# Pairs of steps on TensorE in batches 1 to 3, with batch 0 in float32r throughout

## The chip, the cores and the metric

The kernel runs on one core of one Trainium2 chip. The metric is the time of one execution in device microseconds, measured several times on the chip, with the median taken. A profiled execution is one more execution, whose instructions were recorded; its own time lies among those of the others.

## The reference

`x` has 4 batches of 12416 rows of 128; `inducing` has 32 rows of 128. Each batch goes through two attentions and then through a gated feed-forward part:

```
h   = softmax(inducing @ x.T / sqrt(128)) @ x          # 32 x 128
a   = softmax(x @ h.T / sqrt(128))                     # 12416 x 32
y   = a @ h                                            # 12416 x 128
out = (silu(y @ w_gate) * (y @ w_val)) @ w_out         # w_gate, w_val 128 x 1536, w_out 1536 x 128
```

All data is float32.

## The kernel before

**Tiling.** The 12416 rows of a batch are cut into 25 columns (`COLS`, line 43). Column 0 and the columns of the first three groups have 512 rows, 13 columns in all; the other 12 have 480. The 1536 hidden units are 12 tiles of 128. One **slot** is one tile `t` of one column `c`, so a batch has 300 slots and the kernel 1200. The weights of gate and value are multiplied by `h` beforehand (`proj_round`), so a slot's operand is the softmax itself, laid out as a stack of four 32-row groups (`stack`, 128 x 512).

**A slot.** `front` (line 774) issues two float32r matmuls on TensorE (PE), the gate `g` (line 787) and the value `v` (line 788), each into a PSUM bank of its own from the pool `ps_gv`, which has 6. `gate` (793) makes the silu of `g` on ScalarE (ACT). `value` (801) multiplies it with `v` on VectorE (DVE). The product `h` goes to SBUF (pool `hp`, 3 buffers), except for the tiles in `DVE_TILES` = {1, 5, 9} (in the last batch `LAST_DVE` = {1, 7}), where it overwrites `v` in PSUM. `split` (803) cuts `h` into a rounded high part (a cast, line 814, on ACT, or on DVE for tile 11; in the last batch for tiles 5 and 11) and the rest (a subtraction, line 816, on GpSimd (POOL), or on DVE for the tiles whose `h` lies in PSUM). `back` (820) issues three matmuls `o` into an accumulator from `ps_o` (2 banks): low weights by high part (831), high weights by high part (832), high weights by low part (833). After tile 11 `evac` (837) copies the accumulator on DVE (line 841 or 843) and stores it.

**Types.** From column `CSW` = 13 of batch 0 on (`u.half`, line 778) the two parts and the output weights are float16; before it they are float32r. Float16 needs scales. `peak_of`, `peak_a` to `peak_d` find bounds of the weights, `half_a` to `half_c` make the float16 output weights, `size_a` to `size_d` find each batch's scale, and `rise` (line 474) multiplies batch 0's value weights by the scale, since they were made without it. All this runs as extra steps in slots of batch 0, from the constants in line 63: `WPK` = 104 (bounds), `WSZ` = 128 (scale), `WOH` + 10 = 144 (float16 weights), and slot 146 on for `rise`.

**Order of the work.** The program is unrolled and the order written is the order on each engine. The main loop (lines 881 to 906) does, for each slot: `front`, `gate`, `value` of this tile, then `split` of the tile before it (kept in `wait`), then the extra steps that are due, then `back` of the oldest tiles until no more than `ahead` tiles lie between `front` and `back`. `ahead` is `SKEW` = 5 and rises to `HI` = 10 while the next batch's attention is in the making; at a slot in `bursts`, where ACT computes a long exponential, the tile is split at once and `ahead` falls back, so that PE has a stock of `o` matmuls to work on. The attention of batch b+1 is spread as steps over the slots of batch b (`plan`, line 653). A step whose accumulator comes from `ps_o` has `acc` and waits until the running accumulator isn't about to change (line 899).

Of the kernel before, what the change touches and what calls it, by code (L numbers as in the profile page):

```python
# [9 lines left out]
F32 = mybir.dt.float32  # L10
# [3 lines left out]
ALU = mybir.AluOpType  # L14
AX = mybir.AxisListType
# [27 lines left out]
COLS = [(0, 0)] + [(q, j) for q in range(1, NF) for j in range(NG)]  # L43
SLOTS = len(COLS) * NT
NXT = 4
HI = 10
RAMP = 6
BF = (2, 3, 11, 10)
SKEW = 5
# [10 lines left out]
E0 = 36  # L60
TINY = 2.0 ** -50
LAST_DVE, LAST_CAST = {1, 7}, {5, 11}
WPK, WSZ, WOH, CSW = 104, 128, 134, 13

# [43 lines left out]
def induced_set_attention_then_swiglu(ctx: ExitStack, tc: tile.TileContext, xt, xn, ind, wgv, wo, out):  # L110
# [63 lines left out]
    nc.gpsimd.memset(wide, 2.0 ** 127)  # L174
    peak = const.tile([P, 12], F32, name="peak")
    top = const.tile([P, 36], F32, name="top")
    peaks = const.tile([P, P], F32, name="peaks")

    def floor2(out, in_):

        nc.vector.tensor_scalar(out=out.bitcast(U32), in0=in_.bitcast(U32), scalar1=0x7F800000, scalar2=None, op0=ALU.bitwise_and)
# [7 lines left out]
        at = 6 * k + i  # L189
        nc.vector.tensor_reduce(out=peak[:, at:at + 1], in_=w[:, WP * i:WP * i + WP], op=ALU.max, axis=AX.X, apply_absolute_value=True)  # L190

    def peak_a(k):
        nc.vector.tensor_reduce(out=peak[:, 10 + k:11 + k], in_=peak[:, (0, 6)[k]:(6, 9)[k]], op=ALU.max, axis=AX.X)
        nc.vector.tensor_scalar(out=peaks, in0=ones, scalar1=peak[:, 10 + k:11 + k], scalar2=None, op0=ALU.mult)

    def peak_b(k):
        ps = ps_gv.tile([P, 512], F32, name="gv")
        nc.tensor.matmul(out=ps[:, 0:P], lhsT=peaks, rhs=ident, start=True, stop=True)
        nc.vector.tensor_scalar(out=peaks, in0=ps[:, 0:P], scalar1=TINY, scalar2=None, op0=ALU.max, op1=ALU.max, accum_out=top[:, k:k + 1])

    def peak_c():
        floor2(top[:, 1:2], top[:, 1:2])
        inverse2(top[:, 2:3], top[:, 1:2])

# [5 lines left out]

    def half_a(i):
        cs = slice(WP * i, WP * i + WP)
        joint[i] = sgl.tile([P, WP], F32, name="joint%d" % i)
        nc.gpsimd.tensor_add(out=joint[i], in0=wo_hi[:, cs].bitcast(F32), in1=wo_lo[:, cs].bitcast(F32))

    def half_b(i):
# [53 lines left out]
    def attention(b, one, xn0=None, xt0=None):  # L270
# [180 lines left out]
            nc.vector.tensor_scalar(out=st.hV.bitcast(U32), in0=st.hT[:, 0:M].bitcast(U32), scalar1=0x7FFFFFFF, scalar2=None, op0=ALU.bitwise_and)  # L451

        def size_b():
            ps = ps_gv.tile([P, 512], F32, name="gv")
            nc.tensor.matmul(out=ps[:, 0:M], lhsT=ones, rhs=st.hV, start=True, stop=True)  # L455
            st.sc = att.tile([P, 8], F32, name="sc")
            c = lambda i: st.sc[:, i:i + 1]
            st.up, st.down = c(0), c(1)
            nc.vector.tensor_reduce(out=c(2), in_=ps[:, 0:M], op=ALU.max, axis=AX.X)
            nc.vector.tensor_scalar(out=c(3), in0=c(2), scalar1=top[:, 0:1], scalar2=TINY, op0=ALU.mult, op1=ALU.max)  # L460
            floor2(c(4), c(3))
            inverse2(c(5), c(4))
# [7 lines left out]

        def size_d():
            nc.vector.tensor_scalar(out=st.hV, in0=st.hT[:, 0:M], scalar1=st.up, scalar2=None, op0=ALU.mult)

        def rise(i):

            v = st.w[:, WP * i + 2 * P:WP * i + 4 * P]
            nc.gpsimd.tensor_mul(out=v, in0=v.bitcast(F32), in1=st.up.broadcast_to([P, 2 * P]))

        def weights():
            if not hasattr(st, "w"):  # L480
# [172 lines left out]
    def plan(st, p):  # L653

        f, s = st.f, []

        def add(slot, step, *args):
            def go():
                f[step](*args)


            go.acc = (NT - 1, 0, 1) + (2,) * (step == "hacc") if step in ("s1", "max_b", "hacc", "h_c", "s2") else ()
            s.append((slot, go))

        def blocks(q):
            return CH0[q], CH0[q] + CH[q]

        last = p["S1"][0] + p["S1"][1] * (NCH - 1)
        v1 = last - 3 * p["S1"][1]
        for q in range(NCH):  # L670
            add(p["LX"][0] + p["LX"][1] * q if q < NXT else v1 + 1 + 3 * (q - NXT), "load_xt", q)

            add(v1 if q < NXT else last, "s1", q, q not in (0, NXT))
        mb = last + p["MX"]
        add(last + 2, "max_a"), add(mb, "max_b")
        e1 = mb + p["E1"]
        for q in range(NXN):
            add(e1 - p["LN"][0] + p["LN"][1] * q, "load_xn", q)
            add(e1, "exp1_part", q)
            add(e1, "eT", q)  # L680
            add(e1 + p["HA"][q], "hacc", q, (0, NXN - 1))
        add(e1, "exp1_part", NXN, NCH - 1)
        for q in range(NXN, NCH):
            k = NXN + (q - NXN | 1)
            at = e1 + p["HB"][0] + p["HB"][1] * (k - NXN)
            add(max(at - p["HC"][0] - k + q, e1 + 1 + (p["HB"][0] + p["HB"][1] if q == NCH - 1 else p["HA"][0])), "load_xn", q)
            add(at - p["HC"][1] + 1 - k + q, "eT", q)
            add(at, "hacc", q, (k - 1, k))
        add(at, "h_a")
        add(at + 2, "h_b")  # L690
        hn = at + p["HD"]
        add(hn, "h_c")
        for i, step in enumerate(("size_a", "size_b", "size_c", "size_d")):
            add(hn + 3 * i + 2, step)
        for i, q in enumerate(S2O):
            k = i % NXT
            at = hn + 4 + p["H2"] * (NXT - 1) if i < NXT else hn + p["H2"] * (NCH - 1)
            add(at, "s2", *blocks(q), i not in (0, NXT))
            if i + NXT < NCH:
                add(at + 1, "load_xt", S2O[i + NXT])  # L700
            d = 2 if i < NXT else 1
            add(at + 1 + d * k, "s2_max", *blocks(q))
            add(at + 3 + (d + 1) * k, "s2_sub", *blocks(q))
        e2 = at + 4 + p["E2"]
        add(e2, "exp2")
        st.e1, st.bursts = e1, {e1, e2}
        for i in range(2):
            add(e2 + p["PR"][0], "proj_round", i)
            for k in range(NG * NG):
                add(e2 + p["PR"][i] + 3 + k * p["PQ"], "proj_spread", i, k // NG, k % NG)  # L710
        for q in range(NF):
            first = [u for u, (p, j) in enumerate(COLS) if p == q][0]
            s += post(st, q, nc.gpsimd, SLOTS + NT * (first - NST) + 2, SLOTS)
        return sorted(s, key=lambda x: x[0])
# [146 lines left out]
    for b in range(B):  # L861
        nxt = attention(b + 1, (one, oneb)[(b + 1) % 2]) if b + 1 < B else None
        if nxt is not None:
            nxt.steps = plan(nxt, PA if b == 0 else PB)
            if b == 0:
                cur.steps.append((nxt.e1, lambda: run(f"e2:52:{NTB}")))
                for q in range(2, NF):
                    base = NT * (1 + NG * (q - 1) - NST) + 2
                    base = max(base, E0 + 4) if q < 4 else max(base, nxt.e1 + 1)
                    cur.steps += post(cur, q, nc.gpsimd, base)  # L870
                once = [lambda x=(k, i): peak_of(*x) for k in range(2) for i in range((6, 3)[k])]
                once += [lambda: cur.f["size_a"](), lambda: peak_a(0)]
                cur.steps += [(WPK + 2 * i, f) for i, f in enumerate(once)]
                once = [lambda: peak_b(0), lambda: peak_a(1), lambda: cur.f["size_b"](), lambda: peak_b(1), peak_c, peak_d, cur.f["size_c"]]
                cur.steps += [(WSZ + 2 * i, f) for i, f in enumerate(once)]
                cur.steps += [(WOH + 10 + 2 * i, lambda i=i: (half_a, half_b, half_c)[i // 3](i % 3)) for i in range(9)]
                cur.steps += [(NT * (CSW - 1) + 2 * i + 2, lambda i=i: cur.f["rise"](i)) for i in range(6)]
                cur.steps.sort(key=lambda x: x[0])
        bursts = (nxt.bursts if nxt is not None else set()) | ({E0} if b == 0 else set())
        last_burst = max(bursts, default=0)  # L880
        for slot in range(NT if b == 0 else 0, SLOTS):
            c, t = slot // NT, slot % NT
            u = front(cur, b, c, t)
            gate(u)
            value(u)
            u.cast_dve = t in (LAST_CAST if b == B - 1 else CAST)
            u.last = b == B - 1 and slot == SLOTS - 1
            if wait:
                split(wait[0])
                pend.append(wait.pop(0))  # L890
            wait.append(u)
            if slot in bursts:
                u.cast_dve = True
                split(u)
                pend.append(wait.pop(0))
            for a in (cur, nxt):
                while a is not None and a.steps and a.steps[0][0] <= slot:

                    if pend and pend[0].t in getattr(a.steps[0][1], "acc", ()):
                        break  # L900
                    a.steps.pop(0)[1]()
            ahead = min(ahead + 1 / RAMP, HI) if nxt is not None and slot < last_burst else max(ahead - 1 / RAMP, SKEW)
            if slot in bursts:
                ahead = SKEW - (b == 0)
            while len(pend) + len(wait) > ahead:
                back(pend.pop(0))
        if nxt is not None:
            nxt.steps = [(at - SLOTS, f) for at, f in nxt.steps]
        cur = nxt
# [41 lines left out]
```

## Time and profile before

| | |
|---|---|
| median of 3 runs | 1452.67 us (1452.27 to 1453.83) |
| the profiled execution | 1453.71 us, of which the span from first to last instruction is 1451.9 us |
| mean granted TensorE clock | 0.995 |
| first matmul of batch 0, 1, 2, 3 on line 787 | 38.8, 417.8, 767.2, 1116.5 us from the start of the span |

An instruction's row gives its engine, its line in the kernel, what it writes and reads by tile names, its shapes, how many there were, their busy time and the mean of one in ns, and the idle time just before them with what ended it. Matmuls overlap: the spacing of their starts, not their length, is what one costs in a stream. On ACT and DVE too, the next instruction's start may lie up to 0.1 us before the recorded end of the one before.

### The profile page before, as it was taken

The page shows a single profiled execution, that of the slowest core. Times are in us where ns is not written, and L with a number is a line of the kernel's source. Part 1 is how long each engine was busy: PE and PEld are TensorE (multiplying, and loading weights), DVE is VectorE, ACT ScalarE, POOL GpSimd, SP SyncE. Part 2 cuts the span into 40 slices and gives each one's busy share as a digit, 9 for nine tenths or more (in the row PEclk, how much of TensorE's full clock was granted, in tenths as well). Part 3 has the DMA queues.
Part 4 walks back from the last instruction along what each step waited for, and adds up shares of the span by engine and source line. Part 5 has one row for each costly group of instructions (what it writes and reads, how often), then busy time and mean ns, then how long its engine had stood idle before and what let it go on. Part 6 is the DMA issues. An engine that isn't in the chain of part 4 may idle for free.

```text
span 1451.9 us, 25130 instructions
## 1 busy us (share of the span) xinstructions
PE 1434.0 (99%) x7512; PEld 825.1 (57%) x7512; DVE 1208.2 (83%) x2138; ACT 1266.5 (87%) x2366; POOL 1139.7 (78%) x1036
## 2 busy tenths in 40 slices
PE   9999998999999999999999999999999999999999
PEld 6577776555555555555555455455555555555554
DVE  6888878988888879888888878978888878888887
ACT  4889787789998788899999888799999898889897
POOL 1689768778788667787888767778878889889887
PEclk9999999999999999999999999999999999999999
DMA  9233522212132532121114324221111111111110
GB/s 373 63 98 119 180 87 85 96 52 76 32 111 76 185 129 106 52 70 41 42 36 144 129 88 137 106 74 49 39 42 43 32 42 45 31 44 39 41 42 21
DMA packets 50824, 119.82 MB, mean 83 GB/s; under 512 B 11392, under 2 KB 28288, under 8 KB 50688
## 3 DMA queue, kind: packets, MB, share of 16 engines
q1 hardware_dynamic: 50688, 118.22, 25.0%
q8 instruction: 59, 0.97, 0.3%
q14 instruction: 77, 0.63, 0.1%
HBM read 62.87 MB, written 25.43 MB: 61 GB/s over the span
## 4 chain that ended last, share of the span: by engine, by line
PE 81%; ACT 0%; DVE 0%; issue 0%; DVEq 0%
PE o L831 16%; PE gv L788 16%; PE gv L787 16%; PE o L833 15%; PE o L832 15%; PE gv L329 1%; PE o L377 1%; PE o L329 1%; PE gv L511 0%; ACT silu L793 0%; ACT h_hi L814 0%; DVE ob L841 0%; PE gv L390 0%; PE o L443 0%; PE gv L455 0%
## 5 line engine op out<-in xcount | busy, mean ns | idle before, releaser
L816 POOL TENSOR_TENSOR h_lo<-h,h_hi 128x480 f16<-128x480 f32 (+2 forms) x915 | 1035.4, 1153 | 262.8 <-ACT h_hi L814 185.3
L793 ACT ACTIVATE silu<-gv 128x512 f32<-128x512 f32 (+1 forms) x1200 | 702.8, 587 | 96.4 <-PE gv L787 73.5
L801 DVE TENSOR_TENSOR h<-gv,silu 128x512 f32<-128x512 f32 (+1 forms) x916 | 610.5, 668 | 185.0 <-ACT silu L793 126.3
L787 PE MATMUL gv<-stack,tw 128*128 128x512 f32 (+1 forms) x1200 | 654.1, 545 | 2.2 <-DVE h L801 1.0
L814 ACT CAST h_hi<-h 128x480 f16<-128x480 f32 (+2 forms) x788 | 475.2, 603 | 52.0 <-DVE h L801 45.8
L788 PE MATMUL gv<-stack,tw 128*128 128x512 f32 (+1 forms) x1200 | 466.6, 389 | 3.2 <-DVE h L801 2.3
L831 PE MATMUL o<-h_hi,wo_l 128*128 128x480 f16 (+1 forms) x1044 | 399.0, 382 | 0.0
L832 PE MATMUL o<-h_hi,wo_h 128*128 128x480 f16 (+1 forms) x1044 | 388.2, 372 | 0.0
L833 PE MATMUL o<-h_lo,wo_h 128*128 128x480 f16 (+1 forms) x1044 | 388.2, 372 | 0.0
L787 PEld LDWEIGHTS gv<-stack,tw 128*128 128x128 f32 x1200 | 227.7, 190 | 129.1 <-ACT tw L501 2.7
L831 PEld LDWEIGHTS <-wo_l 128*128 128x128 f16 x1044 | 100.3, 96 | 266.1 <-issue 260.9
L788 PEld LDWEIGHTS gv<-stack,tw 128*128 128x128 f32 x1200 | 227.7, 190 | 39.2 <-ACT silu L793 7.5
L801 DVE TENSOR_TENSOR gv<-gv,silu 128x512 f32<-128x512 f32 (+1 forms) x272 | 184.5, 678 | 30.7 <-ACT silu L793 28.8
L816 DVE TENSOR_TENSOR h_lo<-gv,h_hi 128x480 f16<-128x480 f32 (+2 forms) x272 | 181.0, 665 | 1.4
L833 PEld LDWEIGHTS <-wo_h 128*128 128x128 f16 x1044 | 102.2, 98 | 114.3
L814 ACT CAST h_hi<-gv 128x480 f16<-128x480 f32 (+2 forms) x269 | 153.0, 569 | 10.2 <-DVE gv L801 8.5
L832 PEld LDWEIGHTS <-wo_h 128*128 128x128 f16 x1044 | 104.8, 100 | 3.5
L841 DVE TENSOR_SCALAR ob<-o,sc 128x480 f32<-128x480 f32 (+1 forms) x87 | 62.9, 723 | 0.5 <-PE o L833 0.5
L814 DVE CAST h_hi<-h 128x480 f16<-128x480 f32 (+2 forms) x128 | 61.6, 482 | 0.0
L831 PE MATMUL o<-h_hi,wo_lo 128*128 128x512 f32 x144 | 57.8, 402 | 0.0
L832 PE MATMUL o<-h_hi,wo_hi 128*128 128x512 f32 x144 | 56.6, 393 | 0.0
L833 PE MATMUL o<-h_lo,wo_hi 128*128 128x512 f32 x144 | 56.4, 392 | 0.0
(194 smaller groups left out, 691.3 us busy)
## 6 DMA issues: line engine op xcount, KB each, us to landing
xt_sb<-xt SPq DMA_DIRECT2D x32, 896.0 KB, 5.1
xn_sb<-xn SPq DMA_DIRECT2D x18, 896.0 KB, 5.6
out<-ob SPq DMA_DIRECT2D x52, 256.0 KB, 2.0
out<-ob SPq DMA_DIRECT2D x48, 240.0 KB, 2.0
stack<-a_hi SPq DMA_DIRECT2D x96, 64.0 KB, 2.0
stack<-a_lo SPq DMA_DIRECT2D x96, 64.0 KB, 2.0
stack<-a_hi SPq DMA_DIRECT2D x96, 60.0 KB, 2.0
stack<-a_lo SPq DMA_DIRECT2D x96, 60.0 KB, 2.0
```

The source lines that it names most:

```text
L329: nc.tensor.matmul(out=ps[32 * j:32 * j + 32, 32 * (lo - b0):32 * (hi - b0)], lhsT=lhsT, rhs=st.xt[q][:, lo - CH0[q]:hi - CH0[q], j, :], s ...
L377: nc.tensor.matmul(out=st.hps[32 * g:32 * g + 32, 0:C], lhsT=st.eT[q][:, 32 * i:32 * i + 32], rhs=st.xn[q][:, i, :], start=(tb < NG), stop ...
L787: nc.tensor.matmul(out=u.g[:, :n], lhsT=st.w[:, wcol(0, t)], rhs=rhs, start=True, stop=True)
L788: nc.tensor.matmul(out=u.v[:, :n], lhsT=st.w[:, wcol(1, t)], rhs=rhs, start=True, stop=True)
L793: nc.scalar.activation(out=u.s[:, :u.n], in_=u.g[:, :u.n], func=AF.Silu)
L801: nc.vector.tensor_mul(out=u.h[:, :n], in0=u.v[:, :n], in1=u.s[:, :n])
L814: (nc.vector.tensor_copy if u.cast_dve else nc.scalar.copy)(out=u.hi[:, :n], in_=u.h[:, :n])
L816: eng.tensor_sub(out=u.lo[:, :n], in0=u.h[:, :n], in1=back[:, :n])
L831: nc.tensor.matmul(out=o[:, :n], lhsT=w_lo[:, ws], rhs=u.hi[:, :n], start=(t == 0), stop=False)
L832: nc.tensor.matmul(out=o[:, :n], lhsT=w_hi[:, ws], rhs=u.hi[:, :n], start=False, stop=False)
L833: nc.tensor.matmul(out=o[:, :n], lhsT=w_hi[:, ws], rhs=u.lo[:, :n], start=False, stop=(t == NT - 1))
L841: nc.vector.tensor_scalar(out=ob[:, :n], in0=o[:, :n], scalar1=u.st.down, scalar2=None, op0=ALU.mult)
```

## The change

In batches 1 to 3 the loop takes two slots at a time. It issues `g v g v`, both silus, both products, then the splits, then the steps due in the two slots, then the `back` of (usually) two tiles, six `o` matmuls. Of the splits one tile stays in `wait`, as before, except that none stays at a burst or when the second tile of the pair is one whose `h` lies in PSUM (tiles 1, 5, 9; in the last batch 1, 7): then the tile left over from the pair before and both of this pair are split at once.

Batch 0 goes slot by slot as before but is float32r in all columns (`CSW` = 25), so it needs no scale and no `rise`. The weights' bounds are made from slot 58 on, the two of them in one go with a PSUM bank of `ps_o`; the float16 weights from slot 210 on, one step in four slots, with one SBUF buffer instead of three. `size_b` of the batches takes its bank from `ps_o` and obeys `acc`. `HI` goes from 10 to 9.

```diff
-HI = 10
+HI = 9
-WPK, WSZ, WOH, CSW = 104, 128, 134, 13
+WPK, WOH, CSW = 58, 210, 25
...
-    def peak_a(k):
-        nc.vector.tensor_reduce(out=peak[:, 10 + k:11 + k], in_=peak[:, (0, 6)[k]:(6, 9)[k]], op=ALU.max, axis=AX.X)
-        nc.vector.tensor_scalar(out=peaks, in0=ones, scalar1=peak[:, 10 + k:11 + k], scalar2=None, op0=ALU.mult)
-
-    def peak_b(k):
-        ps = ps_gv.tile([P, 512], F32, name="gv")
-        nc.tensor.matmul(out=ps[:, 0:P], lhsT=peaks, rhs=ident, start=True, stop=True)
-        nc.vector.tensor_scalar(out=peaks, in0=ps[:, 0:P], scalar1=TINY, scalar2=None, op0=ALU.max, op1=ALU.max, accum_out=top[:, k:k + 1])
+    peaks = []
+
+    def peak_a():
+        peaks.append(eTp.tile([P, W], F32, name="eT"))
+        for k in range(2):
+            nc.vector.tensor_reduce(out=peak[:, 10 + k:11 + k], in_=peak[:, (0, 6)[k]:(6, 9)[k]], op=ALU.max, axis=AX.X)
+            nc.vector.tensor_scalar(out=peaks[0][:, P * k:P * k + P], in0=ones, scalar1=peak[:, 10 + k:11 + k], scalar2=None, op0=ALU.mult)
+
+    def peak_b():
+        ps = ps_o.tile([P, 512], F32, name="o")
+        for k in range(2):
+            nc.tensor.matmul(out=ps[:, P * k:P * k + P], lhsT=peaks[0][:, P * k:P * k + P], rhs=ident, start=True, stop=True)
+        nc.vector.tensor_reduce(out=top[:, 0:2], in_=ps[:, 0:2 * P].rearrange("p (k w) -> p k w", k=2), op=ALU.max, axis=AX.X)
...
         def size_b():
-            ps = ps_gv.tile([P, 512], F32, name="gv")
+            ps = ps_o.tile([P, 512], F32, name="o")
...
-        def rise(i):
-
-            v = st.w[:, WP * i + 2 * P:WP * i + 4 * P]
-            nc.gpsimd.tensor_mul(out=v, in0=v.bitcast(F32), in1=st.up.broadcast_to([P, 2 * P]))
...
-                once += [lambda: cur.f["size_a"](), lambda: peak_a(0)]
+                once += [peak_a, peak_b, peak_c, peak_d]
+                peak_b.acc = (NT - 1, 0, 1)
                 cur.steps += [(WPK + 2 * i, f) for i, f in enumerate(once)]
-                once = [lambda: peak_b(0), lambda: peak_a(1), lambda: cur.f["size_b"](), lambda: peak_b(1), peak_c, peak_d, cur.f["size_c"]]
-                cur.steps += [(WSZ + 2 * i, f) for i, f in enumerate(once)]
-                cur.steps += [(WOH + 10 + 2 * i, lambda i=i: (half_a, half_b, half_c)[i // 3](i % 3)) for i in range(9)]
-                cur.steps += [(NT * (CSW - 1) + 2 * i + 2, lambda i=i: cur.f["rise"](i)) for i in range(6)]
+                cur.steps += [(WOH + 4 * i, lambda i=i: (half_a, half_b, half_c)[i % 3](i // 3)) for i in range(9)]
...
-        for slot in range(NT if b == 0 else 0, SLOTS):
+        slot = NT if b == 0 else 0
+        while slot < SLOTS:
             c, t = slot // NT, slot % NT
-            u = front(cur, b, c, t)
-            gate(u)
-            value(u)
-            u.cast_dve = t in (LAST_CAST if b == B - 1 else CAST)
-            u.last = b == B - 1 and slot == SLOTS - 1
-            if wait:
+            us = [front(cur, b, c, t)]
+            if us[0].half:
+                us.append(front(cur, b, c, t + 1))
+            slots = range(slot, slot + len(us))
+            slot += len(us)
+            for u in us:
+                u.cast_dve = u.t in (LAST_CAST if b == B - 1 else CAST)
+                u.last = b == B - 1 and u is us[-1] and slot == SLOTS
+                gate(u)
+            for u in us:
+                value(u)
+            burst = any(x in bursts for x in slots)
+            if burst:
+                us[-1].cast_dve = True
+            late = 0 if burst or us[-1].on_dve and us[-1].half else 1
+            wait += us
+            while len(wait) > late:
                 split(wait[0])
                 pend.append(wait.pop(0))
-            wait.append(u)
-            if slot in bursts:
-                u.cast_dve = True
-                split(u)
-                pend.append(wait.pop(0))
-            for a in (cur, nxt):
-                while a is not None and a.steps and a.steps[0][0] <= slot:
...
-            ahead = min(ahead + 1 / RAMP, HI) if nxt is not None and slot < last_burst else max(ahead - 1 / RAMP, SKEW)
-            if slot in bursts:
-                ahead = SKEW - (b == 0)
-            while len(pend) + len(wait) > ahead:
-                back(pend.pop(0))
+            for x in slots:
+                for a in (cur, nxt):
+                    while a is not None and a.steps and a.steps[0][0] <= x:
...
+                ahead = min(ahead + 1 / RAMP, HI) if nxt is not None and x < last_burst else max(ahead - 1 / RAMP, SKEW)
+                if x in bursts:
+                    ahead = SKEW - (b == 0)
+                while len(pend) + len(wait) > ahead + (slots[-1] - x):
+                    back(pend.pop(0))
```

More of the change, by code (lines that the diff above doesn't have):

```diff
@@ L176, in induced_set_attention_then_swiglu @@
     top = const.tile([P, 36], F32, name="top")
-    peaks = const.tile([P, P], F32, name="peaks")
     def floor2(out, in_):
@@ L190, in peak_of @@
         nc.vector.tensor_reduce(out=peak[:, at:at + 1], in_=w[:, WP * i:WP * i + WP], op=ALU.max, axis=AX.X, apply_absolute_value=True)
-    def peak_a(k):
-        nc.vector.tensor_reduce(out=peak[:, 10 + k:11 + k], in_=peak[:, (0, 6)[k]:(6, 9)[k]], op=ALU.max, axis=AX.X)
-        nc.vector.tensor_scalar(out=peaks, in0=ones, scalar1=peak[:, 10 + k:11 + k], scalar2=None, op0=ALU.mult)
-    def peak_b(k):
-        ps = ps_gv.tile([P, 512], F32, name="gv")
-        nc.tensor.matmul(out=ps[:, 0:P], lhsT=peaks, rhs=ident, start=True, stop=True)
-        nc.vector.tensor_scalar(out=peaks, in0=ps[:, 0:P], scalar1=TINY, scalar2=None, op0=ALU.max, op1=ALU.max, accum_out=top[:, k:k + 1])
+    peaks = []
[9 more added lines that the diff above has]
+        nc.vector.tensor_reduce(out=top[:, 0:2], in_=ps[:, 0:2 * P].rearrange("p (k w) -> p k w", k=2), op=ALU.max, axis=AX.X)
     def peak_c():
+        nc.vector.tensor_scalar(out=top[:, 1:2], in0=top[:, 1:2], scalar1=TINY, scalar2=None, op0=ALU.max)
         floor2(top[:, 1:2], top[:, 1:2])
@@ L212, in half_a @@
         cs = slice(WP * i, WP * i + WP)
-        joint[i] = sgl.tile([P, WP], F32, name="joint%d" % i)
+        joint[i] = sgl.tile([P, WP], F32, name="joint")
         nc.gpsimd.tensor_add(out=joint[i], in0=wo_hi[:, cs].bitcast(F32), in1=wo_lo[:, cs].bitcast(F32))
@@ L659, in go @@
                 f[step](*args)
-            go.acc = (NT - 1, 0, 1) + (2,) * (step == "hacc") if step in ("s1", "max_b", "hacc", "h_c", "s2") else ()
+            go.acc = (NT - 1, 0, 1) + (2,) * (step == "hacc") if step in ("s1", "max_b", "hacc", "h_c", "s2", "size_b") else ()
             s.append((slot, go))
@@ L889, in induced_set_attention_then_swiglu @@
                 split(wait[0])
                 pend.append(wait.pop(0))
-            wait.append(u)
-            if slot in bursts:
-                u.cast_dve = True
-                split(u)
-                pend.append(wait.pop(0))
-            for a in (cur, nxt):
-                while a is not None and a.steps and a.steps[0][0] <= slot:
-                    if pend and pend[0].t in getattr(a.steps[0][1], "acc", ()):
-                        break
-                    a.steps.pop(0)[1]()
@@ L902, in induced_set_attention_then_swiglu @@
-            ahead = min(ahead + 1 / RAMP, HI) if nxt is not None and slot < last_burst else max(ahead - 1 / RAMP, SKEW)
-            if slot in bursts:
-                ahead = SKEW - (b == 0)
-            while len(pend) + len(wait) > ahead:
-                back(pend.pop(0))
+            for x in slots:
+                for a in (cur, nxt):
+                    while a is not None and a.steps and a.steps[0][0] <= x:
+                        if pend and pend[0].t in getattr(a.steps[0][1], "acc", ()):
+                            break
+                        a.steps.pop(0)[1]()
+                ahead = min(ahead + 1 / RAMP, HI) if nxt is not None and x < last_burst else max(ahead - 1 / RAMP, SKEW)
[3 more added lines that the diff above has]
+                    back(pend.pop(0))
```

## The prediction

> **What bounds the kernel now.** I read the page first, then the timeline of PE in a plain stretch, then those of ACT and DVE, and last what PE waited for.
>
> ```profile
> span 1451.9 us, 25130 instructions
> PE 1434.0 (99%) x7512; PEld 825.1 (57%) x7512; DVE 1208.2 (83%) x2138; ACT 1266.5 (87%) x2366; POOL 1139.7 (78%) x1036
> PE 81%; ACT 0%; DVE 0%; issue 0%; DVEq 0%
> ```
>
> PE is busy 99% of the span, and the chain that ended last is PE alone. So TensorE's order sets the time, but ACT at 87% and DVE at 83% have little to spare. The next rows are PE in a plain stretch of batch 3 (480 rows): start, length, line.
>
> ```profile
> 1299.75 0.56 PE L787 MATMUL gv<-stack,tw 128*128 128x480 f32 x1
> ...
> 1301.63 0.37 PE L832 MATMUL o<-h_hi,wo_h 128*128 128x480 f16 x1
> 1301.84 0.37 PE L833 MATMUL o<-h_lo,wo_h 128*128 128x480 f16 x1
> 1301.87 0.56 PE L787 MATMUL gv<-stack,tw 128*128 128x480 f32 x1
> 1302.26 0.38 PE L788 MATMUL gv<-stack,tw 128*128 128x480 f32 x1
> 1302.48 0.38 PE L831 MATMUL o<-h_hi,wo_l 128*128 128x480 f16 x1
> ...
> 1303.99 0.56 PE L787 MATMUL gv<-stack,tw 128*128 128x480 f32 x1
> ```
>
> From 1299.75 to 1303.99 are four slots, 1.06 us each. Line 787 looks dear at 0.56, but its start is recorded 0.03 after that of the `o` ahead of it; what counts is from start to start. From the last `o` to `v` (1301.84 to 1302.26) two matmuls take 0.42, 0.21 each, as `o` to `o` does (1301.63 to 1301.84). From `v` to the first `o` it is 0.22. The change of type costs hundredths, not the 0.18 by which line 787 is longer than line 788.
>
> **Pairs on PE.** A place in batch 1 has two slots' `g v` in a row already (512 rows), and batch 0 has all five matmuls in float32r:
>
> ```profile
> 441.96 0.40 PE L788 MATMUL gv<-stack,tw 128*128 128x512 f32 x1
> 442.19 0.39 PE L787 MATMUL gv<-stack,tw 128*128 128x512 f32 x1
> 442.42 0.39 PE L788 MATMUL gv<-stack,tw 128*128 128x512 f32 x1
> 442.65 0.39 PE L831 MATMUL o<-h_hi,wo_l 128*128 128x512 f16 x1
> ```
> ```profile
> 140.99 0.39 PE L831 MATMUL o<-h_hi,wo_lo 128*128 128x512 f32 x1
> ...
> 142.12 0.39 PE L831 MATMUL o<-h_hi,wo_lo 128*128 128x512 f32 x1
> ```
>
> `v` to `g` and `g` to `v` are 0.23 each; scaled by 480/512 that is 0.215. A pair of 480 is then 0.42 (last `o` to first `v`) + 2 x 0.215 + 0.22 (to the first `o`) + 5 x 0.205 (`o` to `o`) = 2.095, against 2 x 1.06 = 2.12: 0.025 less, uncertain by as much. There are 450 pairs, so PE's own saving is 11 us, between 0 and 22.
>
> Here a rule of the skill can be weighed, first its row: the load of line 831's weights, the first float16 after float32r.
>
> ```profile
> L831 PEld LDWEIGHTS <-wo_l 128*128 128x128 f16 x1044 | 100.3, 96 | 266.1 <-issue 260.9
> ```
>
> These 1044 loads have 266 us of idle time ahead of them that no wait explains, so they are not made early. The Trainium skill (TensorE: Matmul & The Clock Gate, Step-by-step: what each phase is for) says that TensorE pulls weight loads ahead of running matmuls when they go to the background buffer; by it there would be no cost at the seam and pairs would save nothing. The row speaks for a seam.
>
> **What pairs do to ACT and DVE.** This is the part that decides. In the rows below (480 rows, batch 1) DVE's order is product of tile t+1, subtraction of tile t: while ACT casts a tile whose `h` lies in PSUM (766.16), DVE makes the next product (766.35), and the subtraction (766.93) finds the cast done.
>
> ```profile
> 760.75 0.71 DVE L841 TENSOR_SCALAR ob<-o,sc 128x480 f32<-128x480 f32 x1
> ...
> 761.37 0.65 DVE L801 TENSOR_TENSOR gv<-gv,silu 128x480 f32<-128x480 f32 x1
> ...
> 765.69 0.57 ACT L793 ACTIVATE silu<-gv 128x480 f32<-128x480 f32 x1
> 766.16 0.55 ACT L814 CAST h_hi<-gv 128x480 f16<-128x480 f32 x1
> 766.35 0.66 DVE L801 TENSOR_TENSOR h<-gv,silu 128x480 f32<-128x480 f32 x1 [0.45 <-ACT silu L793]
> ...
> 766.93 0.65 DVE L816 TENSOR_TENSOR h_lo<-gv,h_hi 128x480 f16<-128x480 f32 x1
> ...
> 767.49 0.65 DVE L801 TENSOR_TENSOR h<-gv,silu 128x480 f32<-128x480 f32 x1
> ```
> ```profile
> 322.75 0.58 ACT L814 CAST h_hi<-h 128x480 f16<-128x480 f32 x1
> 323.23 0.57 ACT L793 ACTIVATE silu<-gv 128x480 f32<-128x480 f32 x1
> ...
> 1313.20 0.66 DVE L801 TENSOR_TENSOR h<-gv,silu 128x480 f32<-128x480 f32 x1 [0.28 <-ACT silu L793]
> ...
> 1313.89 0.59 ACT L814 CAST h_hi<-h 128x480 f16<-128x480 f32 x1 [0.26 <-DVE h L801]
> ```
>
> In the changed loop a pair whose second tile is 1, 5 or 9 is split at once: on DVE the subtraction stands right behind its own product, must wait for ACT's cast, and the next pair's products queue behind it; on ACT those products' casts queue ahead of the following silus. That closes a ring over two pairs. Take tile 1's cast on ACT as time 0. It lasts 0.55, and a handover is 0.03 (1313.20 + 0.66 to 1313.89) to 0.09 (765.69 + 0.57 to 766.35): DVE's subtraction starts at 0.58 to 0.64. Tile 2's product follows 0.56 later (766.93 to 767.49), at 1.14 to 1.20, lasts 0.65 and hands over in 0.03: ACT casts tile 2 at 1.82 to 1.88, having idled since tile 3's silu. Tile 4's silu follows 0.48 later (322.75 to 323.23), at 2.30 to 2.36; with 0.57 and the handover its product starts at 2.90 to 3.02, tile 5's product 0.58 later (766.35 to 766.93), at 3.48 to 3.60, and 0.66 + 0.03 after that ACT casts tile 5, at 4.17 to 4.29. By ACT alone the silu of 5 and the casts of 3, 4 and 5 follow at 0.47 to 0.48 each, which gives 4.20 to 4.26. So the ring turns in 4.20 to 4.29; I take 4.26, against PE's 2 x 2.095 = 4.19 and the 4.24 of today.
>
> The ring has no slack for anything else on DVE behind such a subtraction. In these columns `back` of tile 11 falls into the pair (4, 5) or (8, 9), so the copy of the accumulator (line 841) joins the ring with 0.62 (760.75 to 761.37). A column of 480 is 3 x 4.26 + 0.62 = 13.40 against 12.72: 0.68 more, between 0.50 and 0.77.
>
> ```profile
> L801 DVE TENSOR_TENSOR h<-gv,silu 128x512 f32<-128x512 f32 x472 | 321.4, 684 | 96.2 <-ACT silu L793 56.8 <-POOL h_lo L816 12.1 <-issue 9.4
> L367 DVE STREAM_TRANSPOSE eT<-s_all 128x448 f32<-128x448 f32 x24 | 15.2, 638 | 1.7 <-ACT s_all L361 1.6
> L339 DVE TENSOR_SCALAR_CACHE_REDUCE s_all<-gv 128x448 f32<-128x448 f32 x18 | 10.7, 620 | 7.6 <-PE gv L329 7.6
> ```
>
> For 512 rows the product is 684 ns against 650 to 660, so I lengthen the ring by 4.5% to 4.45 and the copy to 0.65: 14.00 against 12 x (142.12 - 140.99) = 13.56: 0.44 more, between 0.2 and 0.6. Batches 1 and 2 have 12 columns of 480 and 13 of 512 each: 12 x 0.68 + 13 x 0.44 = 14 us each, between 9 and 17.
>
> The next batch's attention comes on top. Its DVE steps, such as 8 transposes of 0.64 and 6 evacuations of 0.62 a batch in these two forms, are free today. In a pair without such a subtraction a step of up to 0.69 stays free (tile 3's product ends its turn at 2.32, tile 4's starts at 2.96); behind one it is added whole. By the slots of the plan about half fall so, and ACT's two exponentials stop the ring too; PE's own attention matmuls give part back. The two forms are 8.8 us a batch; with half of them added whole, as much again for steps of other forms, and the exponentials against PE's own share, I add 9, an estimate, between 0 and 20. Batches 1 and 2: 2 x (14 + 9) = 46, between 18 and 74.
>
> In batch 3 only tiles 1 and 7 lie in PSUM and tile 5 is cast on DVE, so one ring turn serves six tiles. From tile 4's silu at 2.33, ACT has the silu of 5, the casts of 3 and 4 and the silus of 6 and 7 at 0.47 to 0.48 each; tile 6's silu starts at 4.23 and its product at 4.89, tile 7's product 0.58 later at 5.47, and its cast at 6.16: under PE's 3 x 2.095 = 6.28. There PE's saving stands, 0 to 7 us; POOL, with 10 subtractions a column, may hold it. I take 1.
>
> **Batch 0.** PE's rows with a wait there:
>
> ```profile
> 208.55 0.49 PE L198 MATMUL gv<-ident,peaks 128*128 128x128 f32 x2 [2.97 <-ACT silu L793]
> ...
> 246.96 0.50 PE L788 MATMUL gv<-stack,tw 128*128 128x512 f32 x1 [1.52 <-DVE h L801]
> 253.10 0.46 PE L443 MATMUL o<-fold,hn 128*128 128x128 f32 x2 [1.99 <-DVE hn L398]
> ```
> ```profile
> L816 POOL TENSOR_TENSOR h_lo<-h,h_hi 128x480 f16<-128x480 f32 x443 | 479.9, 1105 | 106.6 <-ACT h_hi L814 74.8 <-DVE h_hi L814 24.5 <-PE o L833 2.3
> L816 POOL TENSOR_TENSOR h_lo<-h,h_hi 128x512 fp32r<-128x512 f32 x108 | 139.1, 1307 | 37.1 <-ACT h_hi L814 28.0 <-DVE h_hi L814 4.8 <-PE gv L788 1.5
> L477 POOL TENSOR_TENSOR tw<-tw,sc 128x256 fp32r<-128x256 f32 x6 | 3.8, 627 | 0.0
> ```
>
> The bounds' matmul (208.55) waits for a `gv` bank while ACT is in the exponential; at slot 58 to 82 and in `ps_o` it doesn't. The waits at 246.96 and 253.10 stand where DVE and POOL carry the float16 weights and `rise` (3.8 us on POOL); these go. That is 6.5 us, and what is late next is PE itself. Against it: 144 slots of 480 go to float32r. Five such matmuls are 1.13 at 512 rows, 1.06 to 1.13 at 480: 0 to 10 us, I take 1, since the spacing scaled by rows is 1.06. POOL's subtraction goes from 1105 to some 1225 (1307 x 480/512), 9 x 1.225 = 11.0 of a column's 12.7 us, and the attention's steps on POOL sit there too: 0 to 5, I take 2. `HI` at 9 takes one `o` step, 3 x 0.21, of cover from each of six exponentials: 0 to 4, I take 1. The weights' bounds and the float16 weights cost the same DVE, ACT and POOL time as before, at slots where PE bounds; if that cover is gone they cost up to their own 10 us. Batch 0: -6.5 + 4 = -2.5, between -6.5 and +13.
>
> **The sum.** The profiled execution took 1453.71, 1.8 more than its span, and stands 1.0 above the median of 1452.67. 1453.7 + 46 - 1 - 2.5 = 1496.2; against the median 1495.
>
> **The rivals.** *PE stays the bound* (0.20). If the ring turns under 4.19, because casts and products follow each other more closely than these rows, the extra steps have slack and pairs pay: 11 us of seams and 2.5 of batch 0, up to 28 in all: 1439, between 1424 and 1447. For it speaks that the ring's lower bound of 4.20 is only 0.01 over PE; against it the copy, which alone is 0.62 in 12.7. *The ring binds only where the plan leaves DVE nothing else* (0.22, part of slower): the attention's steps hide under PE's own matmuls, and the plain columns alone lose. 2 x 14 - 3.5 gives 1477. *No effect* (0.05): the seam costs nothing on PE, as the pulled-ahead weight loads would have it, the ring just keeps up, and only batch 0's waits go: 1450. The forecast has 0.53. The Trainium skill (TensorE: Matmul & The Clock Gate, Architectural detail: the array is 16× 32×32, not 1× 128×128) says that ACT and DVE are strict FIFO; if DVE could let a ready product pass the waiting subtraction, the first rival would hold. The rows here show no overtaking.
>
> **The numbers.** 1495 us is the forecast, with a range of its own of 1468 to 1522 from the bounds above. The range given, 1450 to 1520, takes in the second and third rival and leaves out the first. A measurement of this kernel tells about 0.2%, 3 us, from no change: faster 0.20, the same 0.05, slower 0.75.
>
> **What would show it.** Right: DVE's subtraction (line 816), hardly ever waiting today, gets an idle time of over 100 us released by ACT's casts; ACT's casts wait longer for DVE; PE shows waits of 0.1 to 0.8 on lines 787 and 788 all through batches 1 and 2, released by DVE or ACT, and falls to some 96%; batch 3 keeps its 1.05 to 1.06 us a slot of 480. The wait at line 198 is gone. Wrong: PE still 99% busy, two slots of 480 in under 2.10, and DVE's subtractions without waits.

## The result

The changed kernel takes 1521.33 us (median of 6, 1519.66 to 1522.56) against 1453.25 of the kernel before, a ratio of 1.0468 (1.0454 to 1.0481): slower by 68 us. The forecast was slower by 42, with a range up to 1520, so the direction held, and in batches 1 and 2 the mechanism, and the size lay just outside. From the first matmuls of line 787 in each batch, the batches compare as follows (us; the last from its first such matmul to the end of the span):

| | before batch 0 | batch 0 | batch 1 | batch 2 | batch 3 | span |
|---|---|---|---|---|---|---|
| before | 38.8 | 379.0 | 349.4 | 349.4 | 335.4 | 1451.9 |
| after | 37.3 | 377.7 | 379.5 | 380.5 | 344.5 | 1519.5 |
| difference | -1.5 | -1.3 | +30.1 | +31.1 | +9.1 | +67.6 |

The page of the changed kernel:

```profile
span 1519.5 us, 25146 instructions
PE 1483.4 (98%) x7510; PEld 900.6 (59%) x7510; DVE 1211.2 (80%) x2126; ACT 1248.6 (82%) x2368; POOL 1148.5 (76%) x1029
PE 17%; ACT 2%; DVE 2%; issue 1%; POOL 1%; POOLq 0%; DVEq 0%; ACTq 0%
```

Busy time of PE still reads 98%, and this misleads. Matmuls overlap, so the record of one that starts late still touches the one before it; line 788's weights wait instead. The chain in the last row can't be set beside the 81% of the kernel before: its shares add up to 23% of the span, since here the profile follows the chain back only to 1162.6 us, just ahead of batch 3, and no further. It says next to nothing of batches 1 and 2. The list of waits does (engine, tile and line, what it waited for, us in total, times, the longest):

```profile
ACT h_hi L814 <- DVE h L801: 184.7, 333, 2.1
DVE h_lo L816 <- ACT h_hi L814: 100.4, 178, 1.0
PEld gv L788 <- ACT silu L793: 71.5, 206, 1.1
DVE h L801 <- POOL h_lo L816: 60.1, 105, 0.8
```

The same two instructions in the kernel before (count, then busy time and mean, then the idle time ahead of them):

```profile
L816 DVE TENSOR_TENSOR h_lo<-gv,h_hi 128x480 f16<-128x480 f32 (+2 forms) x272 | 181.0, 665 | 1.4
L814 ACT CAST h_hi<-h 128x480 f16<-128x480 f32 (+2 forms) x788 | 475.2, 603 | 52.0 <-DVE h L801 45.8
```

DVE's subtraction waits 100.4 us for ACT's cast (before, 1.4 us of idle time in all) and ACT's cast 184.7 us for DVE's product (before, 45.8). These two close the ring of the prediction. Two turns of it in a plain stretch of batch 1, columns of 480 rows, first ACT, then DVE, of the timeline (start, length):

```profile
729.23 0.56 ACT L814 CAST h_hi<-gv 128x480 f16<-128x480 f32 x1
729.69 1.04 ACT L793 ACTIVATE silu<-gv 128x480 f32<-128x480 f32 x2
731.08 0.59 ACT L814 CAST h_hi<-h 128x480 f16<-128x480 f32 x1 [0.35 <-DVE h L801]
731.58 1.02 ACT L793 ACTIVATE silu<-gv 128x480 f32<-128x480 f32 x2
732.49 1.08 ACT L814 CAST h_hi<-h 128x480 f16<-128x480 f32 x2
733.55 0.56 ACT L814 CAST h_hi<-gv 128x480 f16<-128x480 f32 x1
...
738.49 0.56 ACT L814 CAST h_hi<-gv 128x480 f16<-128x480 f32 x1
```
```profile
729.82 0.66 DVE L816 TENSOR_TENSOR h_lo<-gv,h_hi 128x480 f16<-128x480 f32 x1 [0.37 <-ACT h_hi L814]
730.40 1.21 DVE L801 TENSOR_TENSOR h<-gv,silu 128x480 f32<-128x480 f32 x2
732.23 0.66 DVE L801 TENSOR_TENSOR h<-gv,silu 128x480 f32<-128x480 f32 x1 [0.62 <-POOL h_lo L816]
732.80 0.66 DVE L801 TENSOR_TENSOR gv<-gv,silu 128x480 f32<-128x480 f32 x1
734.14 0.66 DVE L816 TENSOR_TENSOR h_lo<-gv,h_hi 128x480 f16<-128x480 f32 x1 [0.68 <-ACT h_hi L814]
```

Follow it from 729.23: the cast of tile 1 (0.56), its subtraction at 729.82, tile 2's product at 730.40, its cast at 731.08 after ACT idled 0.35, the silus of 4 and 5 from 731.58, their products at 732.23 and 732.80, the cast of 5 at 733.55. One turn is 4.32 us (forecast 4.26). The wait at 732.23 is put down to POOL, but tile 4's silu, which starts at 731.58 and lasts about 0.56, ends only 0.09 before it: the product waits for the silu. The next turn, 733.55 to 738.49, is 4.94, 0.62 longer, and it holds the accumulator's copy. In 512 rows a turn is 4.53 (forecast 4.45):

```profile
427.20 0.59 ACT L814 CAST h_hi<-gv 128x512 f16<-128x512 f32 x1
431.73 0.59 ACT L814 CAST h_hi<-gv 128x512 f16<-128x512 f32 x1
```

### The profile page after: what moved, and what is told of

Same layout as the page of the kernel before. It is cut to its first block, busy times and chain, and to the rows that moved or that the text cites. A ratio compares the mean times of both kernels' runs of the same rounds, so it can differ in the third digit from the quotient of the medians.

```text
span 1519.5 us, 25146 instructions
## 1 busy us (share of the span) xinstructions
PE 1483.4 (98%) x7510; PEld 900.6 (59%) x7510; DVE 1211.2 (80%) x2126; ACT 1248.6 (82%) x2368; POOL 1148.5 (76%) x1029
## 5 line engine op out<-in xcount | busy, mean ns | idle before, releaser
L816 POOL TENSOR_TENSOR h_lo<-h,h_hi 128x512 f16<-128x512 f32 (+3 forms) x915 | 1049.8, 1167 | 323.4 <-ACT h_hi L814 218.3
L814 ACT CAST h_hi<-h 128x512 f16<-128x512 f32 (+3 forms) x790 | 466.3, 607 | 189.0 <-DVE h L801 184.7
L831 PE MATMUL o<-h_hi,wo_l 128*128 128x512 f16 (+1 forms) x900 | 340.3, 378 | 0.9 <-DVE hn L402 0.9
L833 PE MATMUL o<-h_lo,wo_h 128*128 128x512 f16 (+1 forms) x900 | 335.4, 373 | 1.0 <-POOL h_lo L816 0.9
L832 PE MATMUL o<-h_hi,wo_h 128*128 128x512 f16 (+1 forms) x900 | 335.5, 373 | 0.0
L816 DVE TENSOR_TENSOR h_lo<-gv,h_hi 128x512 f16<-128x512 f32 (+3 forms) x272 | 182.8, 672 | 101.4 <-ACT h_hi L814 100.4
L814 ACT CAST h_hi<-gv 128x512 f16<-128x512 f32 (+3 forms) x269 | 154.1, 573 | 11.8 <-DVE gv L801 5.4
L833 PE MATMUL o<-h_lo,wo_hi 128*128 128x512 f32 (+1 forms) x288 | 111.8, 388 | 0.5 <-POOL h_lo L816 0.5
L831 PE MATMUL o<-h_hi,wo_lo 128*128 128x512 f32 (+1 forms) x288 | 112.2, 390 | 0.0
L832 PE MATMUL o<-h_hi,wo_hi 128*128 128x512 f32 (+1 forms) x288 | 111.0, 386 | 0.0
```

What stands on the lines that cost most here:

```text
L814: (nc.vector.tensor_copy if u.cast_dve else nc.scalar.copy)(out=u.hi[:, :n], in_=u.h[:, :n])
L816: eng.tensor_sub(out=u.lo[:, :n], in0=u.h[:, :n], in1=back[:, :n])
L831: nc.tensor.matmul(out=o[:, :n], lhsT=w_lo[:, ws], rhs=u.hi[:, :n], start=(t == 0), stop=False)
L832: nc.tensor.matmul(out=o[:, :n], lhsT=w_hi[:, ws], rhs=u.hi[:, :n], start=False, stop=False)
L833: nc.tensor.matmul(out=o[:, :n], lhsT=w_hi[:, ws], rhs=u.lo[:, :n], start=False, stop=(t == NT - 1))
```

## The experiments

Each diff is against the changed kernel. Ratios are to the kernel before, measured beside them on the same chip; batch times are worked out as in the table above.

**Pairs undone, the rest kept.**

```diff
-            if us[0].half:
+            if False:
-            late = 0 if burst or us[-1].on_dve and us[-1].half else 1
+            late = 0 if burst else 1
```

> The changed kernel with the pairs undone and all else kept: batches 1 to 3 go slot by slot again (with batch 0 in float32r, the bounds and float16 weights at their new slots, the bank of ps_o, HI at 9). Ring theory (the loss comes from the pair's split at once, which closes a ring of ACT's cast, DVE's subtraction, DVE's next product, ACT's next cast): 1448 to 1454 us, batches 1 and 2 back at 349 us each. Rival A (pairs on TensorE as such cost the time): also near 1450, so this run does not tell those two apart. Rival B (HI at 9, the ps_o bank or the moved weight steps cost it): stays at 1480 to 1521, with batches 1 and 2 at 365 to 380.

Measured: 1450.39 us, ratio 0.998 (0.997 to 0.9989). Batches 377.7, 348.7, 348.7, 335.5. So `HI` at 9, the bank of `ps_o`, and the moved steps cost nothing: the medians differ by 3.6 us in their favour. In the profiled executions 1.4 of that lie in batch 0, 0.6 in each of batches 1 and 2, and 1.3 before batch 0's first slot, which come from the clock and not from the edit (see batch 0 below). All of the loss comes with the pairs or with the rule for the splits. These two had to be parted.

**The split at once, without pairs.**

```diff
-            if us[0].half:
+            if False:
```

> No pairs on TensorE at all (slot by slot in all batches), but the tiles whose h lies in PSUM are split at once, as in the changed kernel. Ring theory: the ring needs no pairs. Worked out as for the change: cast of 5 at 0, its subtraction at 0.59, product of 6 at 1.17, cast of 6 at 1.85 (after the silu of 7), silu of 8 at 2.35, cast of 7, silu of 9 at 3.30, its product at 3.96, its cast at 4.71; a turn of 4.7 us against 4.32, with the accumulator's copy 14.7 us a plain column of 480; batches 1 and 2 at 390 to 405 us each, the time 1535 to 1575. Rival A (pairs on TensorE): 1450, as with the pairs undone.

Measured: 1556.3 us, ratio 1.0713 (1.0693 to 1.0732). Batches 378.8, 389.5, 391.2, 356.8. The ring needs no pairs on TensorE and is worse without them. A plain turn on ACT:

```profile
743.08 0.56 ACT L814 CAST h_hi<-gv 128x480 f16<-128x480 f32 x1 [0.60 <-DVE gv L801]
747.73 0.56 ACT L814 CAST h_hi<-gv 128x480 f16<-128x480 f32 x1 [0.31 <-DVE gv L801]
```

It takes 4.65 us; worked out were 4.71. The turn before it, with the accumulator's copy, takes 4.94, so the copy adds 0.29 here and not the 0.62 expected, and a plain column of 480 rows takes 14.2 us and not 14.7.

**Pairs, with ACT and DVE in the order of single slots.**

```diff
-                gate(u)
-            for u in us:
-                value(u)
...
-            late = 0 if burst or us[-1].on_dve and us[-1].half else 1
-            wait += us
-            while len(wait) > late:
-                split(wait[0])
-                pend.append(wait.pop(0))
+            for u in us:
+                gate(u)
+                value(u)
+                wait.append(u)
+                while len(wait) > (0 if burst and u is us[-1] else 1):
+                    split(wait[0])
+                    pend.append(wait.pop(0))
```

> The changed kernel with TensorE's pairs kept (g v g v, then six o) but ACT, DVE and POOL in the order of single slots: silu and product of the first tile, split of the tile before it, silu and product of the second tile, split of the first; one tile always waits, except at a burst. Ring theory: the subtraction finds its cast done again, so batches 1 and 2 fall to 346 to 350 us each and the time to 1440 to 1452; TensorE's own saving of 0.01 to 0.025 us a pair shows as 5 to 11 us at most. Rival A (pairs on TensorE as such, by having PSUM banks for only one and a half pairs): stays above 1490, with waits of TensorE on the products.

Measured: 1452.19 us, ratio 0.999 (0.9981 to 0.9999), and batches 377.8, 350.7, 350.8, 333.4: time and batches 1 and 2 lie just above the ranges expected. Pairs on TensorE as such don't cost the 68 us, so that rival falls. In batch 3, which has no next batch's attention beside it, they save 335.5 - 333.4 = 2.1 us over 150 pairs against single slots, 0.014 a pair. In batches 1 and 2 they lose 2 us each, within the columns where the next batch's attention runs; why was not tried.

**Pairs, with one tile always left waiting.**

```diff
-            late = 0 if burst or us[-1].on_dve and us[-1].half else 1
+            late = 0 if burst else 1
```

> The changed kernel with one tile always left waiting, also when the pair's second tile lies in PSUM (no split at once except at bursts). Ring theory: the ring over cast and subtraction opens, but the subtraction then comes behind two more products, and tile 5 of the next pair but one wants the bank that tile 1 still holds; worked out, v of the tile after next starts 0.59 us late and the turn of four tiles is about 4.8 us against 4.32, a column about 14.4 to 14.9 us; batches 1 and 2 at 395 to 410 us each, the time 1545 to 1590, slower than the change. If the split at once were the whole harm with nothing in its place: 1450.

Measured: 1448.49 us, ratio 0.9965 (0.9951 to 0.9979). Batches 377.6, 348.4, 348.4, 334.4. My expectation was wrong by about 100 us and the other one written there was right: the split at once was the whole harm, with nothing in its place. PE and DVE of this kernel, a plain stretch:

```profile
702.45 0.56 PE L787 MATMUL gv<-stack,tw 128*128 128x480 f32 x1
...
704.55 0.56 PE L787 MATMUL gv<-stack,tw 128*128 128x480 f32 x1
704.95 0.38 PE L788 MATMUL gv<-stack,tw 128*128 128x480 f32 x1
```
```profile
703.77 1.38 DVE L801 TENSOR_TENSOR h<-gv,silu 128x480 f32<-128x480 f32 x2 [0.56 <-ACT silu L793]
705.06 0.65 DVE L816 TENSOR_TENSOR h_lo<-gv,h_hi 128x480 f16<-128x480 f32 x1
705.87 0.66 DVE L801 TENSOR_TENSOR h<-gv,silu 128x480 f32<-128x480 f32 x1 [0.16 <-ACT silu L793]
```

The subtraction at 705.06 stands behind two products, finds its cast done and waits for nothing; a pair takes 704.55 - 702.45 = 2.10. I had assumed that banks go round in a fixed order, so that `v` at 704.95 would need the bank that the subtraction holds until 705.71. It started before that, so it has another bank, one freed earlier.

**Fewer turns: batch 3's choice of tiles in batches 1 and 2.**

```diff
-        u.on_dve = t in (LAST_DVE if b == B - 1 else DVE_TILES)
+        u.on_dve = t in (LAST_DVE if b > 0 else DVE_TILES)
-                u.cast_dve = u.t in (LAST_CAST if b == B - 1 else CAST)
+                u.cast_dve = u.t in (LAST_CAST if b > 0 else CAST)
```

> The changed kernel with batch 3's choice of tiles in batches 1 and 2 as well: h in PSUM for tiles 1 and 7 only, casts on DVE for tiles 5 and 11. Ring theory: one turn serves six tiles and is under TensorE's time, as in batch 3, where a plain column of 480 took 12.8 us against 13.6; batches 1 and 2 at 355 to 366 us each against 380, the time 1475 to 1498. Rival A (pairs on TensorE as such): within 5 us of 1521.

Measured: 1496.47 us, ratio 1.0295 (1.0281 to 1.0309). Batches 377.4, 367.5, 367.6, 343.8. With two turns a column instead of three, batches 1 and 2 give back 12 to 13 of their 30 us and end 1.5 us a batch above the range expected; the time lies within it. Most plain columns of 480 rows lose nothing any more (12.76 us each on line 787, before 12.72). What is left lies in columns that carry steps of an attention, which batch 3 shows by itself.

**A fourth buffer for `h`.**

```diff
-BF = (2, 3, 11, 10)
+BF = (2, 4, 11, 10)
```

> The changed kernel with four buffers for h in SBUF instead of three. In batch 3 of the changed kernel DVE waited 41 us for POOL to free such a buffer, while the ring of batches 1 and 2 holds no such wait (4 us in its plain columns). Ring theory with POOL as the cause of batch 3's loss: batch 3 goes from 344.5 to 334 to 338 us, batches 1 and 2 stay at 376 to 381, the time 1510 to 1516. Rival: batch 3's 9 us are its own ring's, with the attention's steps in it: batch 3 stays within 2 us.

Measured: 1512.78 us, ratio 1.0413 (1.0399 to 1.0427). Batches 377.1, 379.3, 381.0, 337.0. Batch 3 gets back 7.5 of its 9 us, and batches 1 and 2 nothing. The wait behind it, in batch 3 of the changed kernel and then of this one:

```profile
DVE h L801 <- POOL h_lo L816: 42.7, 66, 0.8
```
```profile
DVE h L801 <- POOL h_lo L816: 10.4, 18, 0.9
```

In batch 3 POOL has 10 of 12 subtractions; with three buffers a product must wait until POOL has read the `h` three of its tiles earlier, and in the pairs' order that wait falls on the ring.

**The ring open, and the bounds' matmul later.** Both kernels have `late = 0 if burst else 1` and the edit below; the second has three buffers for `h`, the first four.

```diff
-                cur.steps += [(WPK + 2 * i, f) for i, f in enumerate(once)]
+                cur.steps += [(WPK + 2 * i + 14 * (i > 9), f) for i, f in enumerate(once)]
```

> One tile always waits, four buffers for h, and the step with the bounds' matmul comes 14 slots later, so that TensorE no longer waits 2.65 and 0.52 us for DVE to make its operands (and then runs at half the rate for 2.5 us). Batch 0 from 377.6 to 372 to 375, batches 1 and 2 at 347 to 349, batch 3 at 313 to 314 for its 24 columns: 1442 to 1446 us, faster than the kernel before by 0.6%.

> As the one before, but with three buffers for h, to tell the later step from the buffer: with the ring open DVE's waits for POOL lie beside TensorE's work, so the fourth buffer is worth 0 to 2 us and this run gives 1443 to 1447 us.

Measured: 1442.97 us with four buffers, ratio 0.9934 (0.992 to 0.9947); 1445.92 with three, 0.9952 (0.9939 to 0.9964). Both beat the kernel before, by 0.7% and 0.5%. Batch 0 takes 374.5 and 375.0, batches 1 and 2 347.3 and 348.4 each. The later step is worth 2.6 us of batch 0 and the fourth buffer about 3 in all, more than the 0 to 2 expected.

## Why the forecast was right in direction and short in size

**Pairs on PE: right.** The seam is a matter of hundredths: 2.10 us a pair of 480 without waits (2.095 forecast), 0.014 a pair measured in batch 3, inside the 0 to 0.05. The rule by which it would cost nothing is near enough that at 450 pairs the difference is 6 us, an estimate from batch 3's 0.014.

**The ring: right, and its turn short by 0.06 to 0.08.** It turns in 4.32 (480) and 4.53 (512). The handover that I took at 0.03 came at 0.09 where tile 5's product meets ACT (732.80 + 0.66 to 733.55), and silu, product and cast each came a hundredth or two later than the plain rows gave. The copy joins the ring with 0.62, as forecast. Three turns and a copy are 13.58 in 480 rows, against 13.40, and the plain columns of 480 rows do take 13.58 on line 787 (before, 12.72). Of the signs named ahead, the subtraction's 100 us, the casts' longer waits and the end of the wait at line 198 came; PE's busy share, which was to fall to some 96%, stayed at 98%.

**The columns with attention: mis-sized in batches 1 and 2.** They lost 61 us where the sum had 46. From line 787's starts, the 12 columns of 480 rows lost 13.7 and 13.4 us (forecast, 8.2 a batch), the 13 of 512 rows 16.4 and 17.8 (forecast, 5.7 and 9 for the next batch's attention). In 480 rows the longer turn explains 12 x 0.18 = 2.2 a batch. Most of the other 3 lies in six columns that carry steps of the second attention, such as its sums, reciprocals and products on DVE and POOL, and take 13.9 to 14.4 each; the sum's 9 was for the next batch's attention alone, and in four of the six the steps are the batch's own. In 512 rows hardly a column is free of attention, so the turn and the steps can't be told apart. None of this was tested by itself. (The step said to stay free in a pair, 0.69, is 0.64 by the two times given for it.)

**Batch 3: the step that failed.** The sum gave it a gain of 1 and it lost 9.1. I had worked out the ring there at 6.16, under PE's 6.28, for a plain column, and named POOL's ten subtractions as something that "may hold it" without working out how. In most plain columns the forecast nearly held: 13.44 to 13.46 us in 512 rows (before, 13.52) and 12.76 in 480 (before, 12.72). But 7.2 of the 9.1 us lie in the ten columns in which the batch's own second attention has steps on DVE and POOL, a term that the sum put at nothing for this batch; another 1.4 lie in the last column. Two such steps on POOL, from two columns that take 13.98 and 14.48 us:

```profile
1212.09 1.05 POOL L559 TENSOR_TENSOR s_all<-s_all,sm 128x512 f32<-128x512 f32 x1
1219.74 1.27 POOL L575 TENSOR_TENSOR a_lo<-aT,a_hi 128x512 fp32r<-128x512 f32 x1
```

The kernel before has the same steps and takes 13.52 in the same columns. With three buffers for `h`, POOL's delay reaches DVE's product and through it the ring. The fourth buffer brings those ten columns from 7.2 to 1.9 and the batch from 9.1 to 1.5, and with the ring open and three buffers they lose nothing against the kernel before: it takes both, the ring and the short supply of buffers.

**Batch 0: the sum near, by errors that cancel.** It gained 1.3 where 2.5 was forecast. The wait for ACT's exponential is gone, as forecast, and another came at the new slot, since the bounds' matmul now follows its own operand on DVE, which is two DVE steps of 0.9 to 1.3 us and had a queue:

```profile
137.09 0.40 PE L788 MATMUL gv<-stack,tw 128*128 128x512 f32 x1
140.14 0.49 PE L202 MATMUL o<-ident,eT 128*128 128x128 f32 x2 [2.65 <-DVE eT L197]
141.15 0.49 PE L202 MATMUL o<-ident,eT 128*128 128x128 f32 x2 [0.52 <-DVE eT L197]
```

2.65 + 0.52 replaces the 2.97 at line 198. "If that cover is gone they cost up to their own 10 us" held the case, but the forecast took the cover as given. Moving the step was worth 2.6 us. Float32r, taken at 1 us, is dearer too: the plain columns of 480 rows take 12.96 us against 12.72, which makes 2.9 over twelve columns, an estimate. On the other side the kernel before lost more at its waits than their length (last section), and that went with them.

The 1.5 us before batch 0's first slot are the execution's and not the change's. They go with the granted clock (third column from the right), here of the kernel before and the changed one:

```profile
33.00:36.00 3.00, 3.00 (x13) 1.59 (x15) 2.64 (x7) 1.68 (x3) 0.47 (x2) 0.55 0.95 328
33.00:36.00 3.00, 3.00 (x42) 1.73 (x40) 2.95 (x8) 2.96 (x7) 0.89 (x2) 1.00 0.98 330
```

The run with batch 3's choice of tiles, whose work up to there is the changed kernel's, had 0.50 in this stretch and its first slot at 39.2; the other runs of this document had 0.76 or more and started at 37.3 to 37.8.

**The rivals.** That PE stays bound would need a turn under 4.19; it is 4.32. That only plain columns lose gave 1477, and the columns of 512 rows, with the next batch's attention, lost more than the others. The misses add up to the 26 us over 1495: 15 in batches 1 and 2, 10 in batch 3 and 1 in batch 0. The range left out 1521.33 by 1.3 us. The bounds of the prediction's terms, added up, run from 1457 to 1540; its own range of 1468 to 1522 was narrower, and the range given stopped at 1520.

## What to carry to other kernels

When the order of an in-order engine is changed, follow one item round the loop, through every engine and back to the first: a wait that costs nothing once becomes the bound if it closes a ring whose turn is longer than the busy engine's time for the same work, and all else on those engines then adds to the turn. An instruction that needs another engine's answer to the one just ahead of it should have other work in between; leaving one tile waiting gave that for nothing and was worth 73 us here. Work the order out for the stretches with extra steps too: batch 3's plain columns came nearly as forecast, and the loss lay in the others. Count the buffers at each handover in the new order too, with the slower of the two engines.

## What the runs showed of the hardware

PE's granted clock halves after a long wait. After the 2.65 and 0.52 us of batch 0 above, matmuls of 512 rows follow each other by 0.43 us instead of 0.23 for some 3.4 us:

```profile
142.73 0.63 PE L788 MATMUL gv<-stack,tw 128*128 128x512 f32 x1
143.16 0.63 PE L831 MATMUL o<-h_hi,wo_lo 128*128 128x512 f32 x1
```

The windows of the changed kernel before, in and after that stretch (PEclk, the granted clock, is the third column from the right):

```profile
130.00:137.00 7.00, 7.00 (x30) 5.24 (x29) 6.72 (x13) 5.80 (x11) 5.31 (x5) 1.00 0.25 75
141.90:144.90 3.00, 3.00 (x9) 2.28 (x8) 2.60 (x5) 1.58 (x3) 1.05 (x2) 0.52 0.02 5
146.00:152.00 6.00, 6.00 (x45) 3.01 (x44) 5.97 (x16) 3.56 (x7) 4.72 (x5) 1.00 0.28 82
```

The granted clock is 0.52 there, so about 3.2 us of waiting cost another 1.6 or so, an estimate from 0.43 against 0.23 over 3.4 us. In the kernel before, the clock after the waits of 2.97 us (208.55), 1.52 (246.96) and 1.99 (253.10) was:

```profile
210.00:213.00 3.00, 3.00 (x56) 2.60 (x48) 1.58 (x6) 1.04 (x2) 2.89 (x3) 0.50 0.59 175
247.40:250.40 3.00, 3.00 (x62) 2.65 (x62) 2.07 (x5) 3.00 (x7) 3.00 (x4) 1.00 0.25 62
254.40:257.40 3.00, 3.00 (x9) 2.40 (x8) 3.00 (x7) 1.65 (x4) 2.90 (x3) 0.50 0.00 0
```

The Trainium skill (TensorE: Matmul & The Clock Gate, Part 1: The HAM clock gate) gives half rate after an idle window of about 3.4 us and full rate after as long a busy one. The length of the slow stretch agrees. The idle time does not: here 1.99 us sufficed, and so did 2.65 and 0.52 with two small matmuls between them. PE's waits in batches 1 and 2 of the changed kernel, the longest of them 1.5 us, left the clock alone: it is 1.00 over both batches.
